# Linear attention and a PReLU MoE in one kernel: the hand-written order of the first three chunks is laid out anew

## The chip, the cores and the metric

The kernel runs on one core of one Trainium2 chip. The metric is the device time of one execution in microseconds, of which the median over runs is compared. Traces come from the hardware profiler, one execution each, and their times count from the first instruction.

## What is computed

The reference has two stages. Lightning attention works on q, k and v of shape (4 batches, 8 heads, 768 rows, 64), in blocks with a decaying state:

```
intra = (q_b k_b^T * Dmask) v_b
inter = (q_b * lam_pow) kv_state
out_b = intra + inter
kv_state = lam^block * kv_state + (k_b * rev_pow)^T v_b
```

The output, seen as 3072 rows of 512, goes through two products with a PReLU between them:

```
h = x @ w_in                               # 512 -> 2048
g = max(h, 0) + alpha * min(h, 0)
out = g @ w_out                            # 2048 -> 512
```

Inputs and the output are float32; the kernel multiplies in float16.

## The kernel before

The rows are cut into six chunks `c`: 256 rows of two batches, 512 rows of the MoE. A chunk holds four attention units, one for each of two batches `bi` and two groups of four heads `hh`; unit n of the list is (c, bi, hh), so chunk 0 has units 0 to 3, with unit 1 = (0, 0, 1) and unit 2 = (0, 1, 0), and chunk 1 has units 4 to 7.

A unit goes through these helpers. `load(c, bi, x, half)` has SP fetch q, k or v; a half load brings one group of heads (256 KB, chunk 0 only), a full load both (512 KB). The raw tiles have five buffers for each of q, k and v. `cast` makes float16 of one operand on ACT (A), DVE (V) or GpSimd, called POOL in the profile (G). `key_decayed` multiplies k by its decay, `transposes` and `transposed` turn q and k, on PE in the opening and by a DMA of SP ("D") later, and `decayed` scales q for the state's part. `cluster(old, new)` issues, in this order on PE: the state's part of unit old, the scores of new, the masked product of old, the key-value products of new; then the masks of new on DVE (`sm`), the copy of old's output into the MoE's input `XT`, and the state's update.

The MoE of a chunk has 16 calls of `up(c, f)`: four products of 128 x 512 with a column block f of w_in, a ReLU on ACT and, in `slope_product`, a multiply-add on DVE that frees the bank of PSUM. It has 16 calls of `down(c, t, part, 4)`: four products each with a quarter of w_out's rows. A `down` with `hold` leaves its store to `store_held`. `fill(n)` issues products that nobody reads.

Weights are fetched by POOL, which also makes float16 of them on the way: `load_win(i)` and `load_wout(i)` bring a quarter each (0.5 MB written, 1 MB read). `gate(i, "in")` is a DMA of one element that reads w_in's quarter i; it stands in SP's queue and so holds what follows in that queue until the quarter has landed.

The schedule is manual: each engine works through its instructions in the order in which the list at the end of the kernel calls the helpers. The list covers chunks 0 to 2; chunks 3 to 5 are woven by a loop (`weave`) of `up` of chunk c with `down` of chunk c - 1 and the attention of chunk c + 1. In the list before, chunk 0's units go through `cluster(None, 0)`, `cluster(0, 2)`, `cluster(2, 1)`, `cluster(1, None)`, `cluster(None, 3)` and `cluster(3, None)`; then come 14 `up` of chunk 0, unit 4, two more `up`, and `down` mixed with units 5 to 7. Of SP's queue, the first entries are twelve half loads, `load(1, 0, "q")`, `gate(1, "in")`, the other five loads of chunk 1, `gate(1, "out")`, `gate(3, "in")`, and then chunk 2's loads.

Of the kernel before, what the change touches and what calls it, by code (L numbers as in the profile page):

```python
# [11 lines left out]
def kernel(  # L12
# [16 lines left out]
    nc = tc.nc  # L29
# [5 lines left out]
    ALU = mybir.AluOpType  # L35

    B, H, S, D = q.shape
    assert (B, H, S, D) == (4, 8, 768, 64)
    L = 128
    W = 2 * L  # L40
    NC = (S // W) * 2
# [28 lines left out]
        for n in range(1, S // L)  # L70
# [24 lines left out]
    def load_win(i):  # L95
        nc.gpsimd.dma_start(  # L96
            out=w_in_sb[:, :, ts(i, 512)],
            in_=moe_w_in[:, ts(i, 512)].rearrange("(g p) f -> p g f", p=128),
        )

    def load_wout(i):
        nc.gpsimd.dma_start(
            out=w_out_sb[:, ts(i, 4), :],
            in_=moe_w_out[ts(i, 512), :].rearrange("(f p) d -> p f d", p=128),
        )
# [73 lines left out]
    )  # L179
    rev_f = const.tile([128, 2], fp32, name="rev_f")  # L180
# [29 lines left out]
    def decay_mask(hp):  # L210
        nc.scalar.activation(dmask[:, :, hp], dmask[:, :, hp], AF.Exp)

# [137 lines left out]
    def cluster(old, new, eng="A", state_first=False, own=False):  # L350

        acc = ps.tile([128, 2, 512], fp32, tag="acc", name="acc")
        ot = [acc[:, a, 0:256].rearrange("p (h i) -> p h i", h=2) for a in range(2)]
        kv = [acc[:, a, 256:384].rearrange("p (h d) -> p h d", h=2) for a in range(2)]
        if own:
            kv = [bank_of("h", "kv")[:, 0:128].rearrange("p (h d) -> p h d", h=2) for a in range(2)]
        if old is not None:
            co, bo, ho = units[old]  # L360
            pbo, bb = co // 2, 2 * (co % 2) + bo
            to = T[old]
            for a in range(2):
                if 2 * pbo + a == 0:
                    continue
                for hp in range(2):
                    nc.tensor.matmul(  # L367
                        ot[a][:, hp, :].rearrange("p (e j) -> p e j", e=2),
                        lhsT=RD[bb, ho][:, a, hp].rearrange("p h d -> p (h d)"),
                        rhs=to["qdT"][:, :, hp, ds(a * 64, 64)],  # L370
                        start=(hp == 0),
                        stop=False,
                        skip_group_check=True,
                    )
        if new is not None:
            c, bi, hh = units[new]
            pb, b = c // 2, 2 * (c % 2) + bi
            t = T[new]
            s = [ps.tile([128, 2, 2, L], fp32, tag=f"s{hl}", name=f"s{hl}") for hl in range(2)]
            for hp in range(2):  # L380
                for e in range(2):
                    for a, hl in QUADS:
                        p = ds(hl * 64, 64)
                        nc.tensor.matmul(  # L384
                            s[hl][ds(a * 64, 64), hp, 1 - e, :].rearrange("p (e j) -> p e j", e=2),
                            lhsT=t["qkT"][p, 1, e, hp, ds(a * 64, 64)],
                            rhs=t["qkT"][p, 0, :, hp, ds(a * 64, 64)],
                            start=True,
                            stop=True,
                        )  # L390
        if old is not None:
            for hp in range(2):
                for e in range(2):
                    for hl, a in QUADS:
                        p = ds(a * 64, 64)
                        nc.tensor.matmul(  # L396
                            ot[a][ds(hl * 64, 64), hp, :],
                            lhsT=to["v16"][p, e, 2 * hp + hl, :],
                            rhs=to["sm"][hl][p, hp, 1 - e, :],
                            start=(2 * pbo + a == 0 and hp == 0 and e == 0),  # L400
                            stop=(e == 1),
                            skip_group_check=True,
                        )
        if new is not None:
            kv_of = [a for a in range(2) if 2 * pb + a + 1 < S // L]
            for hp in range(2):
                for e in range(2):
                    for hl in range(2):
                        for a in kv_of:
                            p = ds(a * 64, 64)  # L410
                            nc.tensor.matmul(  # L411
                                kv[a][ds(hl * 64, 64), hp, :],
                                lhsT=t["kdec"][p, e, 2 * hp + hl, :],
                                rhs=t["v16"][p, e, 2 * hp + hl, :],
                                start=((own or old is None) and hp == 0 and e == 0),
                                stop=(e == 1),
                                skip_group_check=True,
                            )
            t["sm"] = []
            for hl in range(2):  # L420
                sm = sm_pool.tile([128, 2, 2, L], fp16, tag=f"sm{hl}", name=f"sm{hl}")
                nc.vector.tensor_tensor(  # L422
                    out=sm, in0=s[hl], in1=mask_of(hl, hh), op=ALU.mult
                )
                t["sm"].append(sm)

        def output():
            if bo == 0 and ho == 0:
                XT[co] = xt_pool.tile([128, NHP, 2, 2, L], fp16, tag="xT", name="xT")
            copy_on(  # L430
                eng,
                XT[co][:, ds(2 * ho, 2), :, bo, :].rearrange("p h e (a j) -> p a (h e) j", a=2),
                acc[:, :, 0:256].rearrange("p a (he j) -> p a he j", j=64),
            )
            del T[old]

        def state():
            for a in kv_of:
                n = 2 * pb + a
                if n == 0:  # L440
                    for hl in range(2):
                        p = ds(hl * 64, 64)
                        nc.scalar.activation(RD[b, hh][p, 1, :, hl, :], kv[a][p], AF.Copy)  # L443
                    nc.scalar.activation(R[b, hh, 1], kv[a], AF.Copy)  # L444
                    continue
                for hp in range(2):
                    nc.vector.scalar_tensor_tensor(  # L447
                        out=R[b, hh, n + 1][:, hp],
                        in0=R[b, hh, n][:, hp],
                        scalar=rdecay[:, 2 * hh + hp : 2 * hh + hp + 1],  # L450
                        in1=kv[a][:, hp],
                        op0=ALU.mult,
                        op1=ALU.add,
                    )

            for a in range(2):
                if pb == 0:
                    continue
                for hl in range(2):
                    p = ds(hl * 64, 64)  # L460
                    nc.gpsimd.tensor_copy(out=RD[b, hh][p, a, :, hl, :], in_=R[b, hh, 2 * pb + a][p])  # L461

        if old is not None and not state_first:
            output()
        if new is not None:
            state()
        if old is not None and state_first:
            output()
# [60 lines left out]
    def store(c, t, o_ps, c0, n, hold=False):  # L529
# [3 lines left out]
        rows = out[ds(b * S + pb * W, W), ds(c0, n)].rearrange("(j e) d -> e j d", e=2)[t // 2]  # L533
# [60 lines left out]

    query_decay(1, 1)
    key_decay()
    query_decay(0, 1)
    mask_logs(0)
    mask_logs(1)
    decay_mask(1)  # L600
    mask_logs(3)
    mask_logs(2)
    load(0, 0, "k", 0)
    cast(0, "k16", "G")
    key_decayed(0, "V")
    load(0, 0, "q", 0)
    cast(0, "q16", "G")
    fill(4, "h", None, 128)
    transposes(0, "A", False)
    load(0, 0, "k", 1)  # L610
    load(0, 0, "q", 1)
    cast(1, "q16", "A")
    load(0, 1, "q", 0)
    decayed(0, "V")
    cast(2, "q16", "V")
    key_decayed(1, "V")
    load(0, 1, "k", 0)
    cast(2, "k16", "V")
    cast(1, "k16", "G")
    query_decay(2, 1)  # L620
    query_decay(0, 0)
    query_decay(3, 1)
    load(0, 0, "v", 0)
    cast(0, "v16", "G")
    key_decayed(2, "V")
    decay_mask(0)
    fill(5, "h")
    transposes(1, "A", False)
    load_win(0)
    load(0, 1, "q", 1)  # L630
    cast(3, "q16", "G")
    fill(5, "op")
    transposed(2, 1, "V", "h")
    transposed(2, 0, "A", "op")
    decay_mask(3)
    state_decay()
    cluster(None, 0, own=True)
    slopes()
    load(0, 1, "v", 0)
    cast(2, "v16", "A")  # L640
    load_win(1)
    fill(4, "tk")
    cluster(0, 2, "A", own=True)
    load(0, 1, "k", 1)
    cast(3, "k16", "G")
# [302 lines left out]
```

## Time and profile before

| what | before |
|---|---|
| runs | 216.0, 214.21, 214.34 us; median 214.34 |
| span of the profiled execution | 215.6 us |
| PE busy | 206.4 us, 96% |
| DVE, ACT, POOL busy | 131.6, 116.7, 86.8 us |
| moved by DMA | 33.90 MB, mean 157 GB/s |
| SP's queue, POOL's queue of DMAs | 56.6% and 12.1% of 16 engines' span |
| granted clock of PE | 0.998 |

The profiled execution's span runs from its first to its last instruction. Of the three runs only that of 216.0 us is long enough to hold a span of 215.6, so some 0.4 us lie around it. In the profile an engine's busy time is a sum over stages; which engine sets the pace has to be read stage by stage. In the rows of the timeline the number behind a group's start is its length, and the bracket names the idle time before it and what ended it.

### The profile page before, as it was taken

The page shows a single profiled execution, that of the slowest core. Times are in us where ns is not written, and L with a number is a line of the kernel's source. Part 1 is how long each engine was busy: PE and PEld are TensorE (multiplying, and loading weights), DVE is VectorE, ACT ScalarE, POOL GpSimd, SP SyncE. Part 2 cuts the span into 40 slices and gives each one's busy share as a digit, 9 for nine tenths or more (in the row PEclk, how much of TensorE's full clock was granted, in tenths as well). Part 3 has the DMA queues.
Part 4 walks back from the last instruction along what each step waited for, and adds up shares of the span by engine and source line. Part 5 has one row for each costly group of instructions (what it writes and reads, how often), then busy time and mean ns, then how long its engine had stood idle before and what let it go on. Part 6 is the DMA issues. An engine that isn't in the chain of part 4 may idle for free.

```text
span 215.6 us, 5212 instructions
## 1 busy us (share of the span) xinstructions
PE 206.4 (96%) x2089; PEld 107.3 (50%) x2089; DVE 131.6 (61%) x254; ACT 116.7 (54%) x220; POOL 86.8 (40%) x160
## 2 busy tenths in 40 slices
PE   7998997889999999999999999999999999999993
PEld 7564443445444545455554554554545444444453
DVE  7894887664298969879876645745646344444000
ACT  6996787335776544657855545544434534444121
POOL 7285254503592745577677366357311000000000
PEclk9999999999999999999999999999999999999999
DMA  5999999999999999699549997043011011110212
GB/s 164 295 270 206 244 237 249 160 248 281 240 284 144 294 237 271 161 255 173 71 128 227 249 238 203 13 100 97 2 52 49 14 38 49 50 49 3 97 49 97
DMA packets 62478, 33.90 MB, mean 157 GB/s; under 512 B 18150, under 2 KB 59510, under 8 KB 62454
## 3 DMA queue, kind: packets, MB, share of 16 engines
q1 hardware_dynamic: 58182, 29.37, 56.6%
q0 software_dynamic: 4224, 4.19, 12.1%
q8 instruction: 16, 0.26, 0.5%
q14 instruction: 8, 0.07, 0.1%
q10 hardware_dynamic: 48, 0.01, 0.0%
HBM read 27.27 MB, written 6.29 MB: 156 GB/s over the span
## 4 chain that ended last, share of the span: by engine, by line
PE 72%; DMA 20%; SPq 3%; POOL 2%; ACT 1%; issue 1%; DVE 0%; ACTq 0%
PE o_ps L518 30%; PE h_ps L479 29%; PE o_ps L547 6%; DMA vraw<-in_v_dram 5%; DMA kraw<-in_k_dram 5%; DMA w_in_sb<-in_moe_w_in_dram 5%; DMA w_out_sb<-in_moe_w_out_dram 5%; PE s L384 2%; PE acc L396 2%; SPq L87 2%; PE acc L367 2%; PE acc L411 1%; POOL qk L252 1%; ACT o_sb L531 0%; POOL w_in_sb L96 0%
## 5 line engine op out<-in xcount | busy, mean ns | idle before, releaser
L503 DVE SCALAR_TENSOR_TENSOR g<-m,oma,h_ps 128x512 f16<-128x512 f32 x96 | 70.5, 745 | 55.7 <-ACT m L487 54.2
L479 PE MATMUL h_ps<-xT,w_in_sb 128*128 128x512 f16 x384 | 93.4, 379 | 0.6 <-DMA w_in_sb<-in_moe_w_in_dram 0.4
L487 ACT ACTIVATE m<-h_ps 128x512 f32<-128x512 f32 x96 | 56.9, 597 | 50.6 <-PE h_ps L479 49.0
L518 PE MATMUL o_ps<-w_out_sb,g 128*128 128x512 f16 x320 | 79.5, 379 | 2.3 <-DMA w_out_sb<-in_moe_w_out_dram 2.3
L479 PEld LDWEIGHTS <-w_in_sb 128*128 128x128 f16 x384 | 36.5, 98 | 43.5 <-DMA w_in_sb<-in_moe_w_in_dram 0.6
L518 PEld LDWEIGHTS <-g 128*128 128x128 f16 x320 | 30.3, 98 | 38.1 <-DMA w_out_sb<-in_moe_w_out_dram 1.8
L461 POOL COPY RD<-R 64x128 f16<-64x128 f16 x64 | 19.6, 306 | 41.0 <-DVE R L447 39.3
L422 DVE TENSOR_TENSOR sm<-s,dmask 128x512 f16<-128x512 f32 x48 | 30.8, 683 | 7.3 <-PE s L384 7.0
L340 POOL TENSOR_TENSOR qdT<-qkT,qdecay 128x512 f16<-128x512 f16 (+1 forms) x19 | 20.1, 1059 | 11.8 <-ACT qkT L248 6.0
L531 ACT ACTIVATE o_sb<-o_ps 128x512 f32<-128x512 f32 (+2 forms) x26 | 14.7, 564 | 17.8 <-PE o_ps L547 10.9
L248 ACT ACTIVATE xT<-acc 128x512 f16<-128x512 f32 x21 | 12.5, 597 | 12.1 <-PE acc L411 8.1
L278 POOL TENSOR_TENSOR kdec<-kraw,kdecay 128x512 f16<-128x512 f32 x16 | 17.2, 1075 | 3.0 <-DMA kraw<-in_k_dram 3.0
L547 PE MATMUL o_ps<-w_out_sb,g 128*128 128x512 f16 (+2 forms) x96 | 14.1, 308 | 0.0
L447 DVE SCALAR_TENSOR_TENSOR R<-R,rdecay,acc 128x64 f16<-128x64 f16 x56 | 12.3, 272 | 1.2 <-ACT R L444 1.2
L252 POOL CAST qk<-kraw 128x512 f16<-128x512 f32 x12 | 7.4, 613 | 14.1 <-ACT RD L443 9.7
L547 PEld LDWEIGHTS <-g 128*128 128x128 f16 x96 | 8.1, 98 | 6.1
L252 POOL CAST v<-vraw 128x512 f16<-128x512 f32 x13 | 8.2, 628 | 5.3 <-DMA vraw<-in_v_dram 5.2
L396 PE MATMUL acc<-sm,v 64*64 64x128 f16 x384 | 10.0, 217 | 0.2 <-issue 0.2
L384 PE MATMUL s<-qkT 64*64 64x128 f16 x384 | 10.0, 222 | 0.0
L367 PEld LDWEIGHTS <-RD 128*128 128x128 f16 x80 | 6.4, 98 | 5.8 <-ACT RD L443 0.7
L252 POOL CAST qk<-qraw 128x512 f16<-128x512 f32 x13 | 8.0, 616 | 2.2 <-DMA qraw<-in_q_dram 2.0
L367 PE MATMUL acc<-qdT,RD 128*128 128x128 f16 x80 | 8.4, 219 | 0.0
(67 smaller groups left out, 124.2 us busy)
## 6 DMA issues: line engine op xcount, KB each, us to landing
out_dram<-o_sb SPq DMA_DIRECT2D x23, 256.0 KB, 2.5
qraw<-in_q_dram SPq DMA_DIRECT2D x10, 512.0 KB, 5.6
kraw<-in_k_dram SPq DMA_DIRECT2D x10, 512.0 KB, 7.9
vraw<-in_v_dram SPq DMA_DIRECT2D x10, 512.0 KB, 6.0
w_in_sb<-in_moe_w_in_dram POOLq DMA_DIRECT2D x4, 512.0 KB, 9.4
w_out_sb<-in_moe_w_out_dram POOLq DMA_DIRECT2D x4, 512.0 KB, 9.9
kraw<-in_k_dram SPq DMA_DIRECT2D x4, 256.0 KB, 4.3
qraw<-in_q_dram SPq DMA_DIRECT2D x4, 256.0 KB, 4.5
```

The costliest lines, as they stand in the source:

```text
L252: nc.gpsimd.tensor_copy(out=out, in_=in_)
L278: engine(eng).tensor_tensor(out=kdec, in0=kr, in1=kdecay[:, ds(4 * hh, 4), :].rearrange("p h e -> p e h").unsqueeze(3).to_broadcast([128, ...
L340: engine(eng).tensor_tensor(out=qdT[:, :, :, p], in0=(t["qps"] if eng == "P" else t["qkT"][:, 0])[:, :, :, p], in1=qdecay[:, hh, :, :, p], ...
L367: nc.tensor.matmul(ot[a][:, hp, :].rearrange("p (e j) -> p e j", e=2), lhsT=RD[bb, ho][:, a, hp].rearrange("p h d -> p (h d)"), rhs=to["qd ...
L422: nc.vector.tensor_tensor(out=sm, in0=s[hl], in1=mask_of(hl, hh), op=ALU.mult)
L461: nc.gpsimd.tensor_copy(out=RD[b, hh][p, a, :, hl, :], in_=R[b, hh, 2 * pb + a][p])
L479: nc.tensor.matmul(h_ps[:, 0:n] if bi is None else h_ps[:, 0:n].rearrange("p (e j) -> p e j", e=2), lhsT=w_in_sb[:, gi, ts(f, 128)], rhs=x ...
L487: nc.scalar.activation(m[:, 0:n], h_ps[:, 0:n], AF.Relu, scale=-1.0)
L503: nc.vector.scalar_tensor_tensor(out=g, in0=mv, scalar=oma[:, f : f + 1], in1=hv, op0=ALU.mult, op1=ALU.add)
L518: nc.tensor.matmul(o_ps, lhsT=lhs(c, f, t), rhs=w_out_sb[:, f, :], start=(f == 0), stop=(f == NF - 1),)
L531: nc.scalar.activation(o_sb[:, 0:n], o_ps[:, 0:n], AF.Copy)
L547: nc.tensor.matmul(o_ps[:, 0:n], lhsT=lhs(c, f, t), rhs=w_out_sb[:, f, ds(x, n)], start=(f == 0), stop=(f == NF - 1),)
```

## The change

The helpers are cut finer, and the list of chunks 0 to 2 is written anew with them.

`cluster` is split into `carry`, `scores`, `outs` and `keys` (PE) and `masked`, `output` and `state` (the other engines); `pecluster(old, new, own)` calls PE's four in the old order, and the list places `masked`, `output` and `state` by themselves. The loop for chunks 3 to 5 still calls `cluster`, with the instructions of before. In the list every `up` now has its `slope_product` as a call of its own, and every `down` its store apart.

The weights are loaded by block and number of blocks. w_in's first quarter comes in two pieces, the rest in quarters. `keep`, a constant mask, is computed on DVE; the helper `mask_direct` is defined and not called.

```
-    def load_win(i):
+    def load_win(f, n):
         nc.gpsimd.dma_start(
-            out=w_in_sb[:, :, ts(i, 512)],
-            in_=moe_w_in[:, ts(i, 512)].rearrange("(g p) f -> p g f", p=128),
+            out=w_in_sb[:, :, ds(f * 128, n * 128)],
+            in_=moe_w_in[:, ds(f * 128, n * 128)].rearrange("(g p) f -> p g f", p=128),
         )
...
+    keep = const.tile([128, 3, 64], fp32, name="keep")
+    nc.vector.tensor_scalar(out=keep, in0=rel_i, scalar1=0.0, scalar2=None, op0=ALU.is_ge)
...
+    def pecluster(old, new, own=False):
+        if old is not None:
+            carry(old)
+        if new is not None:
+            scores(new)
+        if old is not None:
+            outs(old)
+        if new is not None:
+            if old is None and not own:
+                ACC[new, "own"] = ps.tile([128, 2, 512], fp32, tag="acc", name="acc")
+            keys(new, None if own else (new, "own") if old is None else old)
```

The new list up to the first `up`, with the calls that issue DMAs or that the prediction speaks of (the rest, casts, masks and decays among them, left out):

```
    load(0, 0, "v", 0); load(0, 0, "k", 0); load(0, 0, "q", 0); load(0, 1, "k", 0)
    load(0, 0, "q", 1)
    fill(2, "h", None, 512)
    load(0, 0, "k", 1)
    transposes(0, "V", False)
    load(0, 1, "k", 1)
    pecluster(None, 0, False)
    load(0, 1, "q", 0)
    fill(5, "tk", None, 512)
    load(0, 1, "q", 1)
    cast(2, "q16", "G")
    load(0, 1, "v", 1)
    cast(2, "k16", "G")
    fill(3, "op", None, 512)
    load(0, 1, "v", 0)
    load_win(0, 2)
    load(0, 0, "v", 1)
    fill(2, "tk", None, 512)
    load(1, 0, "q", None)
    load_win(2, 2)
    cast(2, "v16", "V")
    cast(3, "k16", "G")
    pecluster(0, 2, True)
    load(1, 0, "k", None)
    decayed(1, "V")
    cast(1, "v16", "V")
    masked(2, 0)
    decayed(2, "G")
    fill(2, "tk", None, 128)
    masked(2, 1)
    load_win(4, 4)
    load_win(8, 4)
    state(2)
    cast(3, "q16", "V")
    fill(1, "op", None, 512)
    pecluster(2, 1, True)
    fill(1, "op", None, 512)
    load_win(12, 4)
    masked(1, 1)
    load(1, 0, "v", None)
    masked(1, 0)
    transposes(3, "V", False)
    pecluster(1, None, False)
    load_wout(0, 4)
    slopes()
    pecluster(None, 3, True)
    masked(3, 0)
    masked(3, 1)
    pecluster(3, None, False)
    output(3, "V")
    transposed(4, 0, "A", "h")
    up(0, 2, None, "tk", True)
```

Then follow the `up` of f = 0, 3, 1, 4, 7, 6, 11, 8, 10, 5, 14, 13; `transposed(4, 1)`; f = 12; `transposes(5)` and `pecluster(None, 4)`; f = 15 and 9; the parts of `down` (0, 0, 0), (0, 2, 0), (0, 2, 1); `pecluster(4, 5)`; and `down` mixed with units 6 and 7. SP's queue now holds the twelve half loads, all six loads of chunk 1, five loads of chunk 2 and then the first store; its first gate comes after `pecluster(9, 10)`. On POOL `load_wout(4, 4)` stands behind `key_decayed(4)`, and `load_wout(8, 4)` and `load_wout(12, 4)` behind `cast(6, "q16", "G")`.

More of the change, by code (lines that the diff above doesn't have):

```diff
@@ L348 @@
     QUADS = [(x, y) for x in range(2) for y in range(2)]
[L350 to L372, printed above, removed]
+    ACC = {}
@@ L401, in cluster @@
+                            start=(beside in (None, (x, "own")) and hp == 0 and e == 0),
                             stop=(e == 1),
@@ L403, in cluster @@
                         )
[L404 to L458, printed above, removed]
@@ L630 @@
[L630 to L634, printed above, removed]
-    decay_mask(3)
-    state_decay()
-    cluster(None, 0, own=True)
-    slopes()
[L639 to L645, printed above, removed]
-    load(0, 0, "v", 1)
-    decayed(2, "G")
-    cast(1, "v16", "A")
-    load(0, 1, "v", 1)
-    fill(2, "tk")
-    transposes(3, "V", False)
@@ new lines @@
+    load(2, 0, "q", None)
+    cast(7, "k16", "A")
+    down(0, 3, 0, 4, "h", True)
+    cast(6, "k16", "V")
+    decayed(5, "V")
+    slope_product(0, 9, None)
+    output(4, "A")
+    load(2, 1, "k", None)
+    masked(5, 1)
+    transposes(6, "V", False)
+    down(0, 3, 1, 4, "h", True)
+    state(5)
+    load(2, 0, "v", None)
+    query_decay(3, 0)
+    decayed(6, "G")
+    cast(7, "q16", "A")
+    transposes(7, "A", False)
+    decayed(7, "G")
+    down(0, 0, 1, 4, "h", True)
+    masked(5, 0)
@@ new lines @@
+    gate(1, "in")
+    up(2, 13, None, "h", True)
+    slope_product(2, 6, None)
+    decayed(14, "V")
+    pecluster(13, 14, False)
+    masked(14, 0)
+    cast(15, "q16", "A")
+    load(4, 0, "q", None)
+    store_held(1, 2)
+    cast(17, "k16", "V")
+    output(13, "A")
+    slope_product(2, 11, None)
+    slope_product(2, 13, None)
+    load(4, 1, "v", None)
+    transposes(15, "D", False)
+    masked(14, 1)
+    load(4, 1, "q", None)
+    cast(15, "v16", "G")
+    cast(16, "q16", "A")
+    cast(17, "v16", "A")
@@ L907 @@
+    masked(16, 0)
+    transposes(17, "D", False)
+    output(15, "A")
+    up(2, 14, None, "tk", True)
+    cast(18, "k16", "A")
+    slope_product(2, 14, None)
+    cast(18, "q16", "A")
+    key_decayed(18, "G")
+    masked(16, 1)
+    decayed(16, "G")
+    store_held(1, 1)
     for c in range(3, NC):
```

762 lines of the change are left out of this document (451 added, 311 removed).

## The prediction

> **What bounds the kernel now.** I read the page first, then stretches of the span, then PE's own timeline over the opening, then the DMA queues by stretch.
>
> ```profile
> span 215.6 us, 5212 instructions
> 19.60:35.20 15.60, 15.46 (x112) 7.51 (x112) 12.14 (x19) 12.17 (x24) 4.77 (x6) 1.00 1.17 243
> 35.20:49.25 14.05, 11.16 (x199) 6.46 (x200) 8.57 (x19) 4.76 (x11) 5.57 (x8) 1.00 1.07 211
> 49.25:212.00 162.75, 162.53 (x1495) 81.69 (x1489) 94.66 (x173) 83.36 (x147) 63.09 (x116) 1.00 0.59 137
> ```
>
> Each row gives a stretch, its length, then the busy time of PE, weight load, DVE, ACT and POOL, the granted clock, the DMA share and GB/s. From 49.25 us to the end PE idles 0.2 us in 162.75. Nothing is to be won there except fine gaps inside the busy time. The DMA share stands above 1 up to 49 us: the opening is a matter of what the DMA engines bring first. PE's timeline shows where PE paid for that (start, length, last the idle time before the group and its releaser):
>
> ```profile
> 19.68 4.49 PE L479 MATMUL h_ps<-xT,w_in_sb 128*128 128x512 f16 x20 [0.43 <-DMA w_in_sb<-in_moe_w_in_dram]
> 24.01 0.39 PE L326 MATMUL tpx<-ident,qk 128*128 128x128 f16 x4
> 24.23 6.21 PE L479 MATMUL h_ps<-xT,w_in_sb 128*128 128x512 f16 x28
> 32.22 0.61 PE L306 MATMUL tp<-ident,qk 128*128 128x128 f16 x8
> 32.76 0.42 PE L384 MATMUL s<-qkT 64*64 64x128 f16 x16
> 33.24 1.90 PE L479 MATMUL h_ps<-xT,w_in_sb 128*128 128x512 f16 x8
> 36.47 1.04 PE L518 MATMUL o_ps<-w_out_sb,g 128*128 128x512 f16 x4 [1.33 <-DMA w_out_sb<-in_moe_w_out_dram]
> 38.83 0.32 PE L411 MATMUL acc<-v,kdec 64*64 64x64 f16 x16 [0.64 <-POOL v L252]
> 42.28 1.89 PE L518 MATMUL o_ps<-w_out_sb,g 128*128 128x512 f16 x8 [0.33 <-DMA w_out_sb<-in_moe_w_out_dram]
> 44.01 0.28 PE L367 MATMUL acc<-qdT,RD 128*128 128x128 f16 x2
> 44.91 1.04 PE L518 MATMUL o_ps<-w_out_sb,g 128*128 128x512 f16 x4
> 46.59 1.89 PE L518 MATMUL o_ps<-w_out_sb,g 128*128 128x512 f16 x8 [0.65 <-DMA w_out_sb<-in_moe_w_out_dram]
> 49.22 0.39 PE L518 MATMUL o_ps<-w_out_sb,g 128*128 128x512 f16 x1
> ```
>
> The first MoE product starts at 19.68, when the first quarter of w_in lands; after that PE idles 1.33 + 0.64 + 0.33 + 0.65 = 2.95 us, and from 49.22 it never waits again to speak of. At 49.22 PE has done a fixed list: 16 `up` of chunk 0, the attention of units 4 to 7 as far as `cluster(6, 7)`, and 8 of the 16 parts of `down`. Call this the mark. Everything behind the mark is PE's own work, so the change is worth what it does to the time at which PE reaches the same mark.
>
> What the DMA engines can do is read from the queues by stretch, here 8 to 13 us, 18 to 24, and 30 to 33 (packets, MB written, share of 16 engines):
>
> ```profile
> q1 hardware_dynamic: 2936, 1.46, 116.5%
> ...
> q0 software_dynamic: 1210, 1.21, 123.0%
> ...
> q0 software_dynamic: 384, 0.39, 78.0%
> q1 hardware_dynamic: 464, 0.24, 37.0%
> ```
>
> SP's loads (q1) alone run at 0.29 MB/us, so a half load of 0.26 MB takes 0.9 us. The weights (q0) alone run at 202 packets/us: a quarter of w_in, 0.52 MB and some 520 packets, takes 2.6 us. When both queues hold work they take turns, 384 packets against 464, and q0 falls to 128 packets/us: a quarter takes 4.0 us.
>
> **The change, part by part.** *The gates.* Before, the tiny DMA `gate(1, "in")` stands in SP's queue ahead of `load(1, 0, "k")`, and holds every later load until w_in's second quarter is in:
>
> ```profile
> 22.16 0.73 SPq L113 DMA_DIRECT2D gates<-w_in_sb  x1
> 22.94 0.38 SPq L87 DMA_DIRECT2D kraw<-in_k_dram  x1
> ```
>
> That is why q0 had 18 to 24 us to itself. In the new list the first gate, `gate(1, "out")`, comes after unit 10. Behind the twelve half loads SP now issues eleven full loads (chunk 1, most of chunk 2) into free buffers, with no gate and no store between. They are 5.8 MB, 20 us of q1 alone, and they run against all of w_in and half of w_out, so w_in gets the shared rate of 128 packets/us instead of 202. This is the term that decides.
>
> *When w_in starts.* Landing times of the half loads stay, since their number ahead does; only their names change.
>
> ```profile
> 8.12 0.43 DVE L250 CAST qk<-qraw 128x512 f16<-128x512 f32 x1 [0.45 <-DMA qraw<-in_q_dram]
> 9.95 0.62 POOL L252 CAST v<-vraw 128x512 f16<-128x512 f32 x1 [3.21 <-DMA vraw<-in_v_dram]
> 10.51 0.93 POOL L96 DMA_DIRECT2D w_in_sb<-in_moe_w_in_dram  x1
> 11.99 0.77 POOL L96 DMA_DIRECT2D w_in_sb<-in_moe_w_in_dram  x1
> ```
>
> The fifth load of SP's queue lands at 8.1, the seventh at 9.9: 0.9 apart, so the eighth at 10.85, the eleventh at 13.5, the twelfth at 14.4. POOL now issues the first piece of w_in behind `cast(2, "q16", "G")`, which needs the eighth load, and `cast(2, "k16", "G")`: 10.85 + 2 x 0.62 = 12.1, against 10.51. In the old trace almost nothing of q0 moved between its issue at 10.5 and 14.0, and both first quarters (1054 packets) had moved by 20.1, of which the gate of 22.16 tells that the second had landed: 3.5 us from issue to the first packets, 2.0 from the last packet to the landing. The two rows are of 10.5 to 14 us and of 0 to 20.1.
>
> ```profile
> q0 software_dynamic: 2, 0.00, 0.5%
> ...
> q0 software_dynamic: 1054, 1.05, 31.6%
> ```
>
> So the new stream starts at 15.6. The second piece and the other three quarters follow on POOL before 18 us (five issues of 0.77 to 0.93, a cast, one decay), early enough never to leave q0 empty.
>
> *The two pieces.* Each has as many rows as a quarter, half as long. No row shows such a transfer. If bytes count, the pair takes one shared quarter, 4.0 us; if packets count, two, 8.0 us. I take the middle, 6.0. The first `up` of the new list is f = 2, which lies in the second piece, so the split brings no earlier start. The Trainium skill (DMA: Bandwidth & Descriptors, section Queues, rings and completion order) says that each DMA engine takes turns between its queues packet by packet; the 384 against 464 above agree, and by that rule the pair takes the full 8.0 us and the sum below ends 2.0 us later.
>
> *The units.* Order 0, 2, 1, 3 stays, but the last half load is now v of unit 1, and DVE has that unit's cast ahead of the masks of unit 2. From DVE's old rows:
>
> ```profile
> 14.24 0.47 DVE L447 SCALAR_TENSOR_TENSOR R<-R,rdecay,kv 128x64 f16<-128x64 f16 x2 [0.31 <-ACT R L444]
> 14.63 0.68 DVE L250 COPY qkT<-tp 128x1024 f16<-128x1024 f16 x1
> 17.50 1.29 DVE L422 TENSOR_TENSOR sm<-s,dmask 128x512 f16<-128x512 f32 x2 [0.61 <-PE s L384]
> 43.47 0.42 DVE L250 CAST v<-vraw 128x512 f16<-128x512 f32 x1
> ```
>
> 14.45 + 0.42 (cast v) + 1.29 (masks of 2) + 0.47 (state) + 0.43 (cast q of 3) + 1.29 (masks of 1) + 0.68 (qkT of 3) = 19.0; the scores of unit 3 take 0.5 on PE and hide the state of 1; from 19.7 the masks of 3 end at 21.0. Before they ended at 18.8 and the first `up` followed 0.9 later, so attention now allows the first `up` at 21.9, 2.2 us later than before.
>
> *The rest.* No matmul of the model is added. Fewer filling matmuls, one small DVE operation (`keep`), a ninth weight DMA on POOL (0.77) and masks and slope products put elsewhere on DVE cost nothing by themselves, since PE in the opening waits for data, and DVE is 58% busy behind 49 us. If that cover is gone, a slope product that comes late delays the `up` that wants its bank by its own 0.75 us at most.
>
> **The sum.** The last quarter of w_in has landed at 15.6 + 6.0 + 3 x 4.0 + 2.0 = 35.6. Then the new list holds 5 `up`, 4 and 8 transposes, and the scores and keys of unit 4. The pace of pure PE work is in the chain of waits:
>
> ```profile
> 73.69 6.91 PE o_ps L518 x32
> 86.10 4.32 PE h_ps L479 x20
> ```
>
> By these and the starts in PE's timeline: 4.32 + 0.22 + 0.54 + 0.48 = 5.56, to 41.2. Then 8 parts of `down`, three clusters (44.01 to 44.91, 0.90 each) and two groups of 8 transposes: 6.91 + 2.70 + 1.08 = 10.69, to 51.9. The old stretch of 29.54 us (19.68 to 49.22) held 26.0 of work so counted and 2.95 of idle time; 0.6 are small gaps, which I add: 52.45. The mark comes 52.45 - 49.22 = 3.2 us later. The quarters of w_out: the first lands at 33.6 + 4.0 + 2.0 = 39.6, before 41.2; the second at 43.6 against 42.9, up to 0.7 more, left to the range; the last two are issued by POOL behind `cast(6, "q16", "G")`, which waits for q of chunk 1's second batch (about 40), so they land about 50.5 and 54.5, when wanted.
>
> The profiled execution: of the runs of 216.0, 214.21 and 214.34 only the first can hold a span of 215.6, so 0.4 lies around it; 216.0 + 3.2 = 219.2. The median lies 1.66 under that run: **217.5 us**. Pieces at 4.0 and 8.0 give 215.5 and 219.5.
>
> **The rivals.** *Weights first, not slower.* If q0's backlog is served at nearly its own rate, w_in needs 15.6 + 4 x 2.6 + 2.0 = 28.0 for its last quarter and no longer decides; then attention does: 21.9 + 16 `up` at 0.865 + 1.24 + 10.69 + 0.6 = 48.3, a mark 0.9 us earlier, 213.4. For it: the 18 to 24 us row. Against it: 30 to 33 us, where both queues held work. It decides once a quarter takes under 3 us beside SP's loads.
>
> *The long stretch tightens as well.* The 162.75 us hold 672 times 0.216 = 145 us of large matmuls (80 `up`, 352 of `down`) and some 15 clusters of 1.0: 160.4, so up to 2.3 us of fine gaps. If masks and slope products taken out of the clusters remove these on top of the case above: 213.4 - 2.3 = 211.1. Against it: idle time there is already 0.2 us.
>
> *Packets and a slow restart.* Pieces at 8.0 us (+2.0), the second quarter of w_out (+0.7), and PE restarting slowly. At the start of the program PE runs slower than later:
>
> ```profile
> 1.19 1.89 PE L136 MATMUL unread<-RD 128*128 128x128 f16 x16 [1.19 <-DVE RD L118]
> 13.53 0.61 PE L306 MATMUL tp<-ident,qk 128*128 128x128 f16 x8
> ```
>
> 118 ns against 76 ns each. Between 17 and 22 us the new PE has some 2 us of work and two fills fewer; four `up` at 1.5 times their 3.46 us would cost 1.7, half of it hidden under the wait for the next quarter: 217.5 + 2.0 + 0.7 + 0.8 = 221.0. The Trainium skill (TensorE: The Clock Gate, section What's actually happening) puts PE at half clock after an idle window of about 3.4 us; no stretch of this trace is idle that long, so it can't be seen here.
>
> **How the numbers follow.** The forecast has 0.52, spread over 215.5 to 219.5, a fifth of it within 1%. Weights first 0.22, all within 1%. The long stretch 0.10, faster. Packets and restart 0.16. So faster by over 1% (under 212.2; 1% is about what this kernel's measurement can tell from no change) 0.10, within 1% 0.32, slower 0.58. The range goes from the weights-first case to the restart case, 213.4 to 221.0; the forecast's own is 215.5 to 219.5.
>
> **What would show it.** Right: q0 moves under 150 packets/us between 18 and 30 us with q1 active beside it; the first `up` at 22 to 25 us with w_in as its releaser; more idle time of PE on w_in up to 36 us; chunk 1's loads landing earlier than in the old trace for its first batch; PE reaching the mark near 52.5 us; the rest 162 to 163 us long. Wrong: q0 near 200 packets/us with q1 active, a first `up` before 21.5 us, or a mark before 49 us.

## The result, and the profile after

The changed kernel takes 222.5 us, the median of four runs from 221.76 to 223.16, against 214.56 for the kernel before. The ratio is 1.034, with a 95% interval from 1.029 to 1.040: slower by more than the forecast of 217.5, and above the range's upper end of 221.0. The page of the changed kernel's profiled execution (223.16 us in all) shows a longer span, PE busy 1.4 us more than before, and a dent in PE's clock that the page before did not have:

```profile
span 221.0 us, 5176 instructions
PE 207.8 (94%) x2072; PEld 107.0 (48%) x2072; DVE 138.7 (63%) x269; ACT 110.0 (50%) x209; POOL 86.5 (39%) x158
PEclk9999579999999999999999999999999999999999
```

PE's timeline over the opening answers to the one that the prediction read. The four units come late, and no `up` waits for w_in:

```profile
14.28 0.61 PE L340 MATMUL tpx<-ident,qk 128*128 128x128 f16 x8
15.84 0.45 PE L396 MATMUL s<-qkT 64*64 64x128 f16 x16 [0.84 <-DVE sm L408]
18.36 0.42 PE L396 MATMUL s<-qkT 64*64 64x128 f16 x16
20.71 0.23 PE L251 MATMUL at_ps<-ident,alpha_sb 16*128 16x16 f32 x1
22.32 0.42 PE L396 MATMUL s<-qkT 64*64 64x128 f16 x16 [1.38 <-issue]
23.90 0.86 PE L420 MATMUL acc<-sm,v 64*64 64x128 f16 x16
25.09 13.75 PE L539 MATMUL h_ps<-xT,w_in_sb 128*128 128x512 f16 x52
```

The scores of units 2, 1 and 3 start at 15.84, 18.36 and 22.32. Ahead of the last stands an idle time of 1.38 us that nothing in the profile ends ("issue"). The first `up` follows at 25.09, and 52 products take 13.75 us, where 28 of them took 6.21 before. The stretches of the same execution say why (length, then busy PE, weight load, DVE, ACT, POOL, granted clock, DMA share, GB/s):

```profile
20.00:22.00 2.00, 0.80 (x19) 0.61 (x20) 1.29 (x5) 0.96 (x3) 1.08 (x2) 1.00 1.19 229
22.00:23.00 1.00, 0.54 (x32) 0.43 (x31) 0.22 (x1) 0.04 (x1) 1.00 (x3) 1.00 1.20 216
23.00:24.00 1.00, 0.43 (x4) 0.23 (x5) 1.00 (x3) 0.96 (x4) 1.00 (x2) 0.52 1.20 216
25.00:26.00 1.00, 1.00 (x6) 0.45 (x5) 0.49 (x1) 0.58 (x1) 0.98 (x2) 0.50 1.21 219
29.00:30.00 1.00, 1.00 (x4) 0.38 (x3) 0.62 (x1) 0.35 (x1) 0.00 (x0) 0.56 1.20 216
30.00:31.00 1.00, 1.00 (x6) 0.47 (x5) 0.25 (x2) 0.60 (x1) 0.00 (x0) 1.00 1.20 218
```

PE was busy 1.34 us of the 3 before 23, and from 23.0 to 29.9 its granted clock is half. Both DMA queues held work all the while; their rows from 24 to 30 us show the shared rate that the forecast rested on, 857 packets in 6 us, 143 per us:

```profile
q0 software_dynamic: 857, 0.84, 82.9%
q1 hardware_dynamic: 859, 0.43, 35.4%
```

Later in the same timeline two waits are new, on mask products of units 7 and 15:

```profile
59.00 0.42 PE L420 MATMUL acc<-sm,v 64*64 64x128 f16 x16 [0.34 <-DVE sm L408]
111.06 0.42 PE L420 MATMUL acc<-sm,v 64*64 64x128 f16 x16 [0.76 <-DVE sm L408]
```

### The profile page after: what moved, and what is told of

Read it like the earlier page. It is cut to its first block, busy times and chain, and to the rows that moved or that the text cites. A ratio compares the mean times of both kernels' runs of the same rounds, so it can differ in the third digit from the quotient of the medians.

```text
span 221.0 us, 5176 instructions
## 1 busy us (share of the span) xinstructions
PE 207.8 (94%) x2072; PEld 107.0 (48%) x2072; DVE 138.7 (63%) x269; ACT 110.0 (50%) x209; POOL 86.5 (39%) x158
## 4 chain that ended last, share of the span: by engine, by line
PE 78%; DVE 12%; ACT 3%; DMA 2%; issue 2%; SPq 0%; POOL 0%; ACTq 0%; DVEq 0%
PE h_ps L539 32%; PE o_ps L578 28%; PE o_ps L607 6%; DVE g L563 4%; DVE sm L408 4%; PE s L396 3%; PE acc L420 3%; DMA qraw<-in_q_dram 2%; PE acc L378 2%; PE tp L320 1%; DVE R L481 1%; PE acc L444 1%; PE unread L141 1%; DVE kdec L292 1%; DVE qk L264 1%
## 5 line engine op out<-in xcount | busy, mean ns | idle before, releaser
L539 PE MATMUL h_ps<-xT,w_in_sb 128*128 128x512 f16 x384 | 95.4, 387 | 0.1
L539 PEld LDWEIGHTS <-w_in_sb 128*128 128x128 f16 x384 | 37.5, 100 | 45.4 <-issue 3.7
L408 DVE TENSOR_TENSOR sm<-s,dmask 128x512 f16<-128x512 f32 x48 | 31.4, 682 | 7.0 <-PE s L396 5.2
L354 POOL TENSOR_TENSOR qdT<-qkT,qdecay 128x512 f16<-128x512 f16 (+1 forms) x17 | 17.7, 1045 | 13.5 <-DVE qkT L264 7.7
L292 POOL TENSOR_TENSOR kdec<-kraw,kdecay 128x512 f16<-128x512 f32 x18 | 19.4, 1079 | 1.4 <-DMA kraw<-in_k_dram 1.3
L262 ACT ACTIVATE xT<-acc 128x512 f16<-128x512 f32 x17 | 10.1, 596 | 10.1 <-PE acc L444 6.0
L266 POOL CAST qk<-qraw 128x512 f16<-128x512 f32 x8 | 5.2, 661 | 15.9 <-DMA qraw<-in_q_dram 15.9
L266 POOL CAST v<-vraw 128x512 f16<-128x512 f32 x14 | 8.7, 625 | 3.2 <-DMA vraw<-in_v_dram 2.9
L396 PEld LDWEIGHTS <-qkT 64*64 64x64 f16 x384 | 6.5, 108 | 5.9 <-issue 1.8
```

The lines of the kernel that those rows point to most:

```text
L292: engine(eng).tensor_tensor(out=kdec, in0=kr, in1=kdecay[:, ds(4 * hh, 4), :].rearrange("p h e -> p e h").unsqueeze(3).to_broadcast([128, ...
L354: engine(eng).tensor_tensor(out=qdT[:, :, :, p], in0=(t["qps"] if eng == "P" else t["qkT"][:, 0])[:, :, :, p], in1=qdecay[:, hh, :, :, p], ...
L396: nc.tensor.matmul(S[x][hl][ds(a * 64, 64), hp, 1 - e, :].rearrange("p (e j) -> p e j", e=2), lhsT=t["qkT"][p, 1, e, hp, ds(a * 64, 64)], ...
L408: nc.vector.tensor_tensor(out=sm, in0=S[x][y], in1=mask_of(y, units[x][2]), op=ALU.mult)
L539: nc.tensor.matmul(h_ps[:, 0:n] if bi is None else h_ps[:, 0:n].rearrange("p (e j) -> p e j", e=2), lhsT=w_in_sb[:, gi, ts(f, 128)], rhs=x ...
```

## The experiments

**The base again.** 

> The kernel before, unchanged, for a second profile: the shown one has a span of 215.6 us, while the changed kernel's runs stand 2.1 to 2.2 us above their spans. If that holds for the kernel before too, its usual span is about 212.3 us (214.5 - 2.2) and the shown profile was an unusually long execution. Else the span is again near 215.6.

The kernel before took 215.17 us with a span of 213.4. Its timeline:

```profile
17.64 0.41 PE L396 MATMUL acc<-sm,v 64*64 64x128 f16 x14 [0.68 <-DVE R L447]
19.97 4.80 PE L479 MATMUL h_ps<-xT,w_in_sb 128*128 128x512 f16 x20
41.14 1.89 PE L518 MATMUL o_ps<-w_out_sb,g 128*128 128x512 f16 x8 [0.70 <-DMA w_out_sb<-in_moe_w_out_dram]
47.27 3.63 PE L518 MATMUL o_ps<-w_out_sb,g 128*128 128x512 f16 x16
106.15 1.03 PE L518 MATMUL o_ps<-w_out_sb,g 128*128 128x512 f16 x4
```

It reaches the mark at 47.27, not 49.22, with 0.70 us of waits and not 2.95. Span and time lie 1.8 us apart, so the profile shown before, with a span of 215.6, belongs to an execution of some 217.4 us, longer than all three runs listed. This execution is the base below. From the loop's first `down` (at 106.15) to the end the kernels of this table take 106.7 to 107.6 us; the differences lie ahead of it:

| kernel | first `up` | mark | loop's first `down` | span |
|---|---|---|---|---|
| before, e0 | 19.97 | 47.27 | 106.15 | 213.4 |
| changed | 25.09 | 53.2 | 113.49 | 221.0 |
| e2 new opening, old rest | 24.83 | 52.97 | 111.76 | 218.5 |
| e4 small fills | 22.82 | 50.15 | 110.87 | 218.4 |
| e7 mended opening, old rest | 23.48 | 50.91 | 109.70 | 216.5 |
| e11 all mends | 22.96 | 50.66 | 110.23 | 217.8 |
| e12 before without gates | 21.15 | 51.11 | 110.14 | 217.0 |

With the new rest PE has done 12 more products of `down`, 2.6 us, when the same point is reached; the mark is given without them. The changed kernel loses 5.1 us to the first `up`, 0.8 from there to the mark, 1.4 to the loop and 0.3 behind it: 7.6, the difference of the spans.

Each ratio below is to runs of the kernel before that were taken along with the run; their medians lie between 214.8 and 217.1 us. e4, e5, e6, e9, e10 and e14 are one run each, and the four runs of the changed kernel alone lie 1.4 us apart, so what is read from these six is their traces.

**Which half of the list.** The old list as far as its first `up`, then the new rest: 

> The list of before up to cluster(3, None), then the new list from the first up on (v of chunk 1's first batch, the first quarter of w_out and the cast of unit 4's q put between). Theory 'opening' (the loss is the late first up and PE's half clock after it): 214 to 217 us, first up near 19.7 us at full clock. Theory 'rest' (the finely cut list behind the opening costs the most): 219 us or more. My forecast's theory (w_in served beside SP's loads): 214 to 216, since the gate is kept here.

The new list as far as unit 3's output, then the old rest: 

> The new list up to the output of unit 3, then the list of before from its first up on. Theory 'opening': 219 to 223 us, with the granted clock again near 0.5 for some 6 us after 23 us. Theory 'rest': 214 to 217 us. Forecast's theory (w_in): 218 or more with PE waiting on w_in.

They took 223.43 us (ratio 1.027, from 1.009 to 1.045) and 219.37 (1.015, from 1.004 to 1.026). The new opening is dear with either rest, and e2's clock was at half from 22.45 to 29.28, as "opening" had it. The first pairing shows only that the new rest doesn't fit the old opening's loads: PE waits 3.01 us for w_out and 1.48 for v there.

**Half clock.** Fifteen more filling products between the units: 

> The changed kernel with 15 more filling products of 128x512 between units 2, 1 and 3 (17 to 23 us), where PE was idle. Theory 'clock' (PE's idle time lowers its clock to a half from 23.0 to 29.6 us, which costs 6.6 x 0.5 = 3.3 us): granted clock 1.0 throughout and 219 us, 3 us less than the changed kernel. Theory 'w_in' (the weights bound the first products anyway): 222 us, the saved time returning as waits on w_in.

```
-    fill(1, "op", None, 512)     # twice, around pecluster(2, 1)
+    fill(4, "op", None, 512)     # and 2, with 2, 5 and 3 more further on
```

222.31 us (1.030, from 1.020 to 1.040). The clock stayed at 1.00 from 20 to 40 us, and 52 products took 11.57 us instead of 13.75: the half clock costs 2.2 us. But the first `up` moved to 27.43, and the gain was gone: 1.1 us of the delay stood already ahead of the first added fill (unit 2's scores at 16.92), and 1.3 came behind it.

The first of these goes with the clock too. The trace's own record of the clock begins with the first grant of full clock, at 15.16 us in this run, at 12.80 in the changed kernel and at 7.05 in e0. Ahead of that grant the rows print 1.00, but PE's products have the length of half clock: 20 of 128 columns took 2.32 us at 9.11 in e4, whose rows print 1.00 there, and 2.17 at 12.79 in e7, whose rows print 0.50. These are five filling products of 512 columns in the changed kernel and in e0:

```profile
9.35 2.31 PE L141 MATMUL unread<-ident 128*128 128x512 f16 x5
8.51 1.24 PE L141 MATMUL unread<-ident 128*128 128x512 f16 x5
```

With its fewer fills PE was busy for 0.32 us from 4 to 6 us and for 1.15 from 6 to 8 in the changed kernel, against 2.00 and 1.79 in e0.

**The stop.** The 12 early fills of 512 columns as 48 of 128: 

> The changed kernel with its first four fills (12 products of 128x512) written as 48 products of 128x128: same columns, 72 more instructions in PE's stream. In the kernel before, in the changed one and in e2 and e3 PE stops with no releaser in sight at the same place of its stream, behind instruction 442 or so (0.2 to 0.7 us before; 1.4, 1.7, 1.5 us here), some 6.2 to 6.6 us after it passed instruction 187, which is 256 earlier. Theory 'instruction supply' (a block of 256 instructions takes over 6 us to arrive while the DMA engines are full, and the new list runs through 256 of them in 5 us): the stop of 1.4 us ahead of the scores of unit 3 goes, and the first up comes 1 to 1.5 us earlier, near 23.8 us; span 219 to 220. Theory 'hidden data wait': the stop stays at the scores of unit 3.

```
-    fill(5, "tk", None, 512)
+    fill(5, "tk", None, 128)     # and three more like it
```

PE's timeline of this run:

```profile
22.82 6.38 PE L539 MATMUL h_ps<-xT,w_in_sb 128*128 128x512 f16 x28
30.04 5.50 PE L539 MATMUL h_ps<-xT,w_in_sb 128*128 128x512 f16 x24 [0.85 <-DMA w_in_sb<-in_moe_w_in_dram]
```

220.55 us. The stop is gone, the clock never falls, the first `up` comes 2.3 us earlier, and now PE meets the forecast's wait on w_in.

The same in the kernel before: 

> The kernel before, with nothing changed but that its 23 filling products of 512 columns are issued as 92 of 128 columns, the same time on TensorE in four times as many instructions. Theory 'instruction supply' (TensorE stops at a fixed count of its instructions because the next block of them has not landed yet): the block boundaries now fall 69 instructions later in the work and more instructions' time lies ahead of each, so the stop of 0.19 to 0.68 us without releaser behind the scores of the first units disappears and the median is 0.2 to 0.7 us below the kernel before (ratio 0.997 to 0.999). Rival 'the stop is the gate or a load': the stop stays where it is and the ratio is 1.000.

217.39 us, ratio 1.011 (from 1.008 to 1.015): the wrong sign. The timeline shows two waits, which are half of it (the loop's first `down` comes 1.5 us later than in e0; another 1.2 us behind it stay unexplained), and it settles the mechanism better than a gain would have:

```profile
14.21 0.42 PE L384 MATMUL s<-qkT 64*64 64x128 f16 x16
18.72 0.53 PE L396 MATMUL acc<-sm,v 64*64 64x128 f16 x8
20.21 0.31 PE L396 MATMUL acc<-sm,v 64*64 64x128 f16 x8 [0.96 <-issue]
59.89 0.42 PE L384 MATMUL s<-qkT 64*64 64x128 f16 x16 [1.01 <-DMA qkT<-qk]
```

Counted along the timeline, PE stops behind its 222nd product in both traces of the kernel before, in the changed one and in e1, e2, e5, e9 and e12 (in e3 behind the 223rd), whatever work that is. Here it passes the 222nd at 14.4 without a stop and stops behind the 350th. That is 128 products and as many weight loads later: 256 instructions. From 256 instructions ahead of the stop to the restart it took 6.0 us in the first trace, 6.3 in the changed kernel, 7.3 in e12 (from the 94th product) and 5.8 here (from the 222nd), with the DMA engines full. The page of the changed kernel has a queue whose transfers fit:

```profile
q8 instruction: 16, 0.26, 0.5%
```

These are 16 packets of 16 KB for PE's 4144 products and weight loads, one for every 259. The trace has the time of each. In the ten traces with a stop one such packet ends 1.3 to 1.6 us before PE goes on: at 15.31 for 16.86 in the first trace, at 20.93 for 22.32 in the changed kernel, at 17.04 for 18.46 in e12, at 18.68 for 20.21 here. In seven traces without a stop, and here at the 222nd product, it ended 1.7 us or more before PE came there. So PE waits for its next block of instructions, and that block comes by DMA, beside the loads.

**The mask.** `decay_mask(1)` right behind `decay_mask(0)`: 

> The changed kernel with the exponential of the second decay mask right behind the first on ACT, where the old place lay behind other ACT work and the first mask product waited 1.74 us for it (12.8 to 14.5). Theory 'mask': the first mask product starts at 12.8, and the products of unit 2 and the first up come up to 1 us earlier. Theory 'loads' (v of units 2 and 1 set the pace, 13.5 and 14.4 us): first up unchanged within 0.3 us.

221.75 us, the first `up` at 24.92: refuted, the stop (1.43 us) stayed. The masks of unit 0 ran 2.0 us earlier, but the scores of unit 2 only 0.15, now released by ACT's copy of that unit's transposes:

```profile
15.69 0.42 PE L396 MATMUL s<-qkT 64*64 64x128 f16 x16 [0.84 <-ACT qkT L262]
```

The span is 219.6; the clock was at half for 3.4 us here and not for 6.8.

**The gate.** `gate(1, "in")` and `load(1, 0, "k")` put back behind w_in's third load: 

> The changed kernel with the gate on w_in's second quarter again ahead of all of chunk 1's loads but the first. My forecast's term (w_in at the shared rate decides): the weights run at about 200 packets/us from 16 to 24 us, the first up comes earlier and the span falls by 2 us or more. Theory 'units and clock' (PE never waited for w_in in the changed kernel): weights land earlier but the first up stays near 25 us and the span within 1 us of 221, or it grows where chunk 1's loads come late.

221.4 us. The queues from 18 to 24 us show w_in alone on the DMA engines, 196 packets/us:

```profile
q0 software_dynamic: 1175, 1.16, 118.3%
```

The stop vanished here too, so loads without a gate also delay PE's instructions: the packet of the next block ended at 18.95, 1.9 us before PE came there. The first `up` came at 23.27, and the clock never fell. The span of 219.3 is 1.7 us below the changed kernel's, between the figures of the two theories; later waits on w_out (1.07 us) and on the cast of v (0.45) took most of what the full clock gave back.

**The forecast's terms alone.** The kernel before with its three gates left out: 

> The kernel before without its three gates, nothing else changed. This measures the forecast's deciding term by itself: the list of before, TensorE at its first up product at 20.0 us, and the loads of chunk 1 running beside the weights. Theory 'shared packets decide': w_in moves at about 143 packets/us instead of 195, TensorE waits 2 to 4 us on w_in_sb between 24 and 37 us, and the median is 216.5 to 218.5 (ratio 1.009 to 1.019). Rival 'the shared rate is hidden' (as in the changed kernel, where no wait on w_in is seen): no wait on w_in above 0.5 us and a ratio of 0.998 to 1.003.

218.48 us, ratio 1.013, from 1.006 to 1.020. PE's timeline and the queues from 24 to 30 us:

```profile
18.46 0.41 PE L396 MATMUL acc<-sm,v 64*64 64x128 f16 x14 [1.53 <-issue]
21.15 4.76 PE L479 MATMUL h_ps<-xT,w_in_sb 128*128 128x512 f16 x20 [0.29 <-DMA w_in_sb<-in_moe_w_in_dram]
28.48 2.76 PE L479 MATMUL h_ps<-xT,w_in_sb 128*128 128x512 f16 x12 [0.62 <-DMA w_in_sb<-in_moe_w_in_dram]
32.25 1.90 PE L479 MATMUL h_ps<-xT,w_in_sb 128*128 128x512 f16 x8 [1.00 <-DMA w_in_sb<-in_moe_w_in_dram]
44.86 1.89 PE L518 MATMUL o_ps<-w_out_sb,g 128*128 128x512 f16 x8 [1.61 <-DMA w_out_sb<-in_moe_w_out_dram]
q0 software_dynamic: 778, 0.77, 75.2%
q1 hardware_dynamic: 1182, 0.60, 43.7%
```

130 packets/us of weights, 1.9 us of waits on w_in, 0.9 more on w_out than e0, 0.85 more at the instruction stop: 3.65 us, where the spans differ by 3.6. With PE on time the shared queue has its price: 2.8 us of waits on weights and a longer stop.

The kernel before with `load_win(0)` as two loads of 256 columns: 

> The kernel before with w_in's first quarter loaded in two pieces of 256 columns, nothing else changed. Theory 'pieces are nearly free': 528 packets more on the weights' queue, under 0.5 us later for the last quarter, which PE meets with slack: ratio 0.998 to 1.003. Rival of the forecast (pieces dear, up to 2.0 us more): waits on w_in of 0.5 to 2.0 us and a ratio of 1.003 to 1.010.

215.49 us, ratio 1.002, from 0.999 to 1.006: no difference.

**The late masks.** `masked(7, 0)` and `masked(15, 0)` right behind `masked(7, 1)` and `masked(15, 1)`: 

> The changed kernel, with the mask products masked(7,0) and masked(15,0) issued right behind masked(7,1) and masked(15,1), ahead of the copies and slope products that VectorE did before them. Theory 'masks' (the new rest costs 1.3 to 1.9 us because TensorE waits for these two products): the two waits on DVE sm of 0.34 and 0.76 us go, the span falls by 1.1 to 1.7 us to 219.3 to 219.9, and from the end of the part before chunk 2's last cluster to the first down product of the loop it is 1 us shorter than in the changed kernel. Rival 'order of the list as such': the waits move to another tile and the span stays at 220.5 to 221.3.

The idle times of its PE timeline behind the mark:

```profile
86.70 0.42 PE L396 MATMUL s<-qkT 64*64 64x128 f16 x16 [0.41 <-DMA qkT<-qk]
110.77 0.31 PE L444 MATMUL kv<-v,kdec 64*64 64x64 f16 x8 [0.20 <-DVE g L563]
111.42 1.89 PE L539 MATMUL h_ps<-xT,w_in_sb 128*128 128x512 f16 x8 [0.35 <-DVE g L563]
```

222.68 us, span 220.8. Both waits went and 0.96 us of others came: of 1.10 us, 0.2 were won. So these two masks are not the new rest's price by themselves; what is stays open.

**Mends together.** Old rest with e4's and e5's edits: 

> The kernel of e2 (new opening, old list behind it) with both mends of e4 and e5. Theory 'opening': its 5 us over the kernel before are the units' late end and the half clock, so that the first up moves from 24.8 to about 22.5 us, and if PE is kept busy enough the clock stays up: 215 to 217 us; with the clock still falling 217 to 218. Theory 'loads': 219.

218.54 us (1.013, from 1.006 to 1.019), the best of the new openings, but above both figures of "opening". PE's clock was at half from 7.81 to 14.64 us in this execution, and unit 2's scores came at 16.36, where e4 has them at 15.37.

New rest, e4's and e5's edits, and unit 2 served first: 

> The changed kernel with the fills in small products as in the run before that had them, and unit 2 served first: its q is the fifth load instead of the eighth, its casts and transposes stand ahead of unit 1's keys, the first decay mask is made earlier. Theory 'order of the units' (unit 2's late q and late transposes hold the four units back): the first up product starts at 21.0 to 21.8 us instead of 22.8, the waits on w_in grow from 0.9 to 1.5 to 2.5 us, and the span is 217.4 to 218.4. Rival 'loads' (v and the later k set the pace): first up at 22.6 to 23.0 and the span 218.2 to 218.8.

```
+    load(0, 1, "q", 0)           # fifth load instead of eighth
+    cast(2, "q16", "G")          # ahead of key_decayed(1, "G"), with its k16
+    transposed(2, 0, "A", "h")   # ahead of fill(5) and transposes(1)
```

The same with e9's edit: 

> The run before (small fills, unit 2 served first, first mask earlier) and the two late mask products moved forward. If the four causes found (instruction supply, unit 2's place, half clock, late masks) are all there is beside the shared packet rate, the median is 217.0 to 218.0, a ratio of 1.011 to 1.016 to the kernel before, and what is left are waits on w_in of 1.5 to 2.5 us between 22 and 36 us. If the new opening has another fault that none of these touch, it stays at 219 or above. If w_in's waits vanish too and the median is below 215.5, the shared packet rate costs nothing and the forecast's deciding term is refuted.

220.47 us, and 220.34 (1.028, from 1.021 to 1.035). The first `up` stayed at 23.2 and 22.96: the order of the units as edited here was not the limit. The wait on w_in went, and one of 1.6 us on w_out came at 50 us.

e11 with unit 1's transposes behind unit 2's scores, then also the loads in the order 0, 2, 1, 3: 

> The run with all mends, and on TensorE unit 1's transposes moved behind unit 2's scores and unit 0's outputs. Theory 'order on TensorE' (in that run unit 2's keys and queries are transposed by 11.4 us but its scores start at 15.58, behind unit 1's transposes and the fills that wait for their copy): unit 2's scores start at 12.5 to 14 us and the first up product at 21.0 to 22.0 instead of 22.96. Rival 'loads' (unit 2's v lands only at 13.8 and unit 1's behind it): scores early, but its key products wait for v until 14.2 or later, and the first up product stays at 22.5 to 23.2.

> The run before (unit 2's scores ahead of unit 1's transposes) and the twelve loads of chunk 0 put in the order in which units 0, 2, 1, 3 need them: v k q of 0, then k q v of 2, of 1 and of 3. If the order of list and loads is what holds the first up product at 23 us, it now starts at 20.0 to 21.5, the shared packet rate decides (waits on w_in and w_out of 2 to 4 us in all up to 50 us), and the median is 216.5 to 218.0. If TensorE's chain of four units one behind the other (2.4 us each by ACT's state copies) is the limit, the first up product is at 21.5 to 22.5 and the median 217.5 to 219.5. Below 215 would refute the shared rate as a cost.

e14's timeline, scores of units 2, 1 and 3 and the first `up`:

```profile
14.20 0.42 PE L396 MATMUL s<-qkT 64*64 64x128 f16 x16
19.21 0.42 PE L396 MATMUL s<-qkT 64*64 64x128 f16 x16
22.37 0.64 PE L396 MATMUL s<-qkT 64*64 64x128 f16 x16
24.97 11.57 PE L539 MATMUL h_ps<-xT,w_in_sb 128*128 128x512 f16 x52
```

220.53 us, and 220.95 (1.025, from 1.018 to 1.032). In e14 unit 2's scores came 1.4 us earlier, but unit 1's 1.2 later and the first `up` 2.0 later, in e15 2.6 later (25.52): both theories missed. The half clock was back in both, from 19.76 to 23.18 in e14 and from 19.07 to 22.48 in e15. What holds the four units 3 us behind the old list once the stop is away stays open. The traces point at two things that no run changed: PE's half clock at the start, which lasts until 12.94 us in e14 and 13.91 in e11, and ACT, for whose copy of unit 0's output PE waits ahead of unit 1's scores (0.67 us in the changed kernel, 0.71 in e11, 1.22 in e14). No order tried here reached 20 us, and no version beat the kernel before.

## Why the prediction was wrong, step by step

*The base.* The step "only the first can hold a span of 215.6, so 0.4 lies around it" failed. It is 1.8 us around e0's span and 2.16 around the changed kernel's, and the profiled execution was not among the runs shown. Subtracting 1.66 from it took out a lead that the changed kernel's own profiled run (0.66 over its median) did not have. These are 1.76 and 1.0 us of the error of 5.0.

*The deciding term.* "w_in gets the shared rate" was right in size (128 packets/us forecast, 143 and 130 measured) and has a price where PE is on time (e12), but it did not decide: in the changed kernel no product waits for w_in, as PE is later still. The stream began at about 15.6 as worked out, at first slowly (27 packets before 16.6), and the pair of pieces took about 5 us (954 of its 1054 packets had moved by 20.0), between the bounds and below the 6.0 taken. By the packet rule of the Trainium skill (DMA: Bandwidth & Descriptors, Queues, rings and completion order) the pair was to take 8.0; the even counts of 857 and 859 agree with turns by packet. But half-long packets moved faster: 315 beside 325 of SP's queue from 18.5 to 20.0, some 210 per us of each.

*The units.* "attention now allows the first `up` at 21.9" is the term that failed: 25.09. The sum went along DVE's queue from 14.45 and took the masks of unit 2 to follow at once, at 14.87. They ran at 16.93, behind the masks of unit 0, two casts and `decayed(1)`. That is 2 us; the stop is 1.4 more, and no term of the sum had it, though the trace before held one of 0.19. Two rows of the changed kernel show what the sum along DVE alone left out:

```profile
14.53 1.29 DVE L408 TENSOR_TENSOR sm<-s,dmask 128x512 f16<-128x512 f32 x2 [1.74 <-ACT dmask L213]
14.70 1.08 ACT L262 ACTIVATE qkT<-tpx 128x512 f16<-128x512 f16 x2 [0.20 <-PE tpx L340]
```

The masks of unit 0 waited for ACT and ended at 15.82, and ACT's copy of unit 2's transposes ended at 15.78; PE issued the scores of unit 2 at 15.84. As e5 took the first of the two away and won 0.15 us, the second holds them just as long. It runs back over PE and ACT: POOL had the casts of unit 2 done at 12.24, but PE transposed them at 14.28, behind a fill that waited for ACT's copy of unit 1's transposes (12.77 to 13.79), and those PE had issued at 11.72, behind five fills at half clock. This chain is read from the trace; no run takes it apart.

*The clock.* "A slow restart" was a rival, at 1.7 us half hidden. It cost 2.2 us, not hidden (e3). The Trainium skill (TensorE: Matmul & The Clock Gate, What's actually happening) has the clock halve after an idle window of about 3.4 us; here PE was still busy in 45% of the 3 us before. The 6.8 us of half clock are two of its free-running windows, which agrees. "Fewer filling matmuls" stood among what would "cost nothing by themselves"; with them PE had full clock 5.75 us later than in e0. Five fills and unit 1's transposes took 1.5 us longer at half clock (2.31 and 1.01 us) than e0's five fills and the prediction's row of 0.61 for eight transposes; how much of that reaches the first `up` no run shows.

*The mark and the rest.* The mark came at 53.2 against 52.45, but from the wrong base and for other reasons, so that it fits is luck: against e0's 47.27 it is 5.9 us later, nearly twice the 3.2 of the sum. That the rest would cost nothing failed by 1.4 us from mark to loop, 1.16 of it idle time of PE. Mark 0.75, rest 1.4 and base 2.76 make 4.9 of the 5.0 us between 217.5 and 222.5.

## What to carry to other kernels

Ask of each engine when it arrives before pricing the transfer that it may wait for: a wait that is real by itself (e12) is worth nothing behind a later one, and comes back when that is mended (e4). Make the base a pair of span and time of one and the same execution, and repeat it if its waits are not those of the runs compared. In an opening where every engine hands on to the next, sum the chain through all of them, not the queue of the one that looks longest. Before a fill is taken out, ask what keeps PE's clock up in its place.

## What had not been expected of the hardware

PE can run out of instructions. Where small products come fast and the DMA engines are full, it stops at a fixed count of its own stream, 0.2 to 1.7 us long, 256 instructions apart, and the profile names no releaser or a chance one. The Trainium skill (Runtime: NRT & Kernel Launch, Instruction fetch mechanics) has blocks of 256 instructions too, and calls the cost of crossing one "mostly hidden"; with DMA engines full it is not.

PE's clock goes by windows. In each of the 18 traces kept here the changes of clock lie a whole number of 3.41 us apart. Cut into such windows from the first grant, they agree on what decides. At full clock, PE was busy for 23 to 52% of the 8 windows that half clock followed, and no window that kept it was under 49%. At half clock, it was busy for 81 to 100% of the 26 windows that full clock followed, and for 26 to 85% of the 30 others. The windows don't begin with the program: e4 and e7 have the same first fills, and full clock came at 11.86 us in one, and at 4.40 and again at 14.64 in the other.
